# Four output projections as 64-row matmul pairs that change sides behind a wait on POOL

## Chip, core and metric

The kernel runs on one core of a Trainium2 chip. TensorE (PE) multiplies a stationary operand, loaded by a weight load (PEld), with a moving operand, and writes into one of eight PSUM banks; VectorE (DVE) and ScalarE (ACT) read PSUM; GpSimd (POOL) works beside them; SyncE (SP) issues most transfers. The metric is device microseconds (us) of one execution; lower is better.

## What is computed

Decayed linear attention over blocks of 64 positions (batch 2, 8 heads, 768 positions, head size 64), and then two feed-forward layers over its output x of 1536 tokens by 512. All are float32.

```python
h = x @ w_in                                   # 512 -> 2048
g = where(h >= 1, h, where(h <= -1, 0, (h + 1)**2 / 4))
x = g @ w_out                                  # 2048 -> 512
gate = 1 / (1 + exp(-(x @ w_gate)))            # 512 -> 1536
out = (gate * (x @ w_val)) @ w_out2            # 1536 -> 512
```

## The kernel before

Every float32 operand of a feed-forward matmul is split into a high and a low part (fp32r), and a product is three matmuls: high by high, high by low, low by high. The hidden width is cut into slices of 128: n = 0 to 15 of the first layer, n = 16 to 27 of the second (NF1 = 16, NF2 = 12). The 1536 tokens are three tiles t of 512 (NTT = 3). For each slice and tile the kernel makes the hidden values (gate and value products, tiles named h, p or t in the profile), their activation (gh, the high part, and gl, the low one), and then the output projection, `project`, which multiplies that slice's 512 tokens by its 128x512 piece w of the output weight.

A projection has four PSUM banks, accs[0] to accs[3] (a in the profile), one for each 128 tokens of the tile. For each bank it issues three matmuls of 128 rows, 128 columns of stationary operand and 512 moving columns: gh by w high, gh by w low, gl by w high. Two slices (GF = 2) accumulate into the same four banks; after the second one `flush` adds each bank to the tile `part[t]` in SBUF, one DVE addition of 128x512 per bank in the order j = 0 to 3 (L336), and for the last two slices SP sends each 128x512 piece to the output as soon as its addition is done (L339).

The banks of these accumulations come from a PSUM pool of four buffers, so that a projection of the next tile that starts anew (first) writes the same four banks, and each of its first matmuls waits for the DVE addition that reads that bank. The order on every engine is written out by hand. At the end of the program it is, on TensorE: the projections of slices 26 and 27 for tile 0, mixed with products; then, with nothing between them, (26, t=1), (27, t=1), (26, t=2), (27, t=2). Here (27, t=1) ends an accumulation and (26, t=2) begins the next one in the same four banks. After (27, t=2) come only four additions and four output transfers.

Two other parts of the program matter to the prediction. In the attention, `scores` (L980) multiplies operands of 64 rows for two heads, one in rows 0 to 63 and one in rows 64 to 127, in turn, each into a bank of its own; `values` (L1041) and `queries` (L1061) use the array in halves in other ways. And POOL makes sums of weights (L163) for the second layer, in a stretch that ends long before the last projections.

Of the kernel before, what the change touches and what calls it, by code (L numbers as in the profile page):

```python
# [15 lines left out]
B, H, S, D = 2, 8, 768, 64  # L16
# [9 lines left out]
NF1, NF2 = FF1 // P, FF2 // P  # L26
G0 = 4
GF = 2
# [17 lines left out]
def fused_kernel(ctx: ExitStack, tc: tile.TileContext, qkv, qd, cst, w1, w2, out):  # L46
    nc = tc.nc
    pe, act, dve, pool, sp = nc.tensor, nc.scalar, nc.vector, nc.gpsimd, nc.sync
# [10 lines left out]
    def bank(name, use="h"):  # L59
        pool_ = banks.get(use) or banks[None]  # L60
        return pool_.tile([P, 512], F32, tag="b", name=name)
# [178 lines left out]
    def w_need(n, o):  # L240
        while index[n, o] not in ws:
            k = prog["round"]
            w_round()
            assert prog["round"] > k
# [49 lines left out]
        dve.scalar_tensor_tensor(out=r, in0=r, scalar=1.0, in1=h, op0=ALU.min, op1=ALU.max)  # L294

    accs = {}

    def project(n, t, gs, first, last, now=True):
        gh, gl = gs
        two = n >= NF1  # L300
        o = 1024 if two else 512
        w_need(n, o)
        w = ws[index[n, o]]
        if first:
            accs.update({j: bank(f"a{n}_{t}_{j}", "a") for j in range(4)})
        for j in range(4):
            js = slice(j * P, (j + 1) * P)
            if two:
                ah, al = (g[j] if isinstance(g, list) else g[:, js] for g in (gh, gl))
                ops = [(ah, w[:, 0]), (ah, w[:, 1]), (al, w[:, 0])]  # L310
            else:
                ops = [(w[:, 0, js], gh), (w[:, 1, js], gh), (w[:, 0, js], gl)]
            for m, (a, b_) in enumerate(ops):
                pe.matmul(accs[j], lhsT=a, rhs=b_, start=(first and m == 0),  # L314
                          stop=(last and m == 2))
        if t == NTT - 1:
            used.update([index[n, o]] if two else [index[n, 0], index[n, o]])
        if last and now:
            flush(n, t)
# [4 lines left out]
    def flush(n, t, js=range(4)):  # L324
        two = n >= NF1
        begin = n == (NF1 + GF if two else G0) - 1
        end = n == (NF1 + NF2 if two else NF1) - 1
        for j in js:
            o = part[t][:, j]
            if begin:  # L330
                if j < 2 or (n, t) == (G0 - 1, 0):
                    act.activation(o, accs[j], AF.Copy)  # L332
                else:
                    dve.tensor_copy(out=o, in_=accs[j])
            else:
                dve.tensor_tensor(out=o, in0=o, in1=accs[j], op=ALU.add)  # L336
            if end and two:
                r0 = t * TT + j * P
                sp.dma_start(out=out[r0:r0 + P, :], in_=o)  # L339
# [24 lines left out]
    def feed_forward():  # L364
        def finish():
            project(*behind.pop(0))
            if u is not seq[-1]:
                w_round()
            if u in seq[4:6]:
                w_round()  # L370

        for u in seq:
            n, t, first, last = u
            h = hidden(n, t, 0)
            if u not in seq[1:G0]:
                split()
            yield
            r = act1(h, n, t)
            act1_end(r, h)
            fresh.append((u, r))  # L380
            yield
            j = seq.index(u)
            while attention_over and len(behind) >= (4 if j < NEARLY else 3 if j < 8 else 2):
                finish()
        split()
# [226 lines left out]
    def first_layer(waiting, made):  # L612

        square = lambda s: act.activation(s, s, AF.Square)
        for n0 in range(G0, NF1, GF):
# [18 lines left out]
            act1_end(s11, r[0])  # L634
            s22 = act1_begin(r[2], f"s{n1}_1")
            project(*waiting[0], now=False)
            square(s22)
            g11 = parts(s11, n0, 0)
            act1_end(s22, r[2])
            w_round()  # L640
            project(*waiting[1], now=False)
            g22 = parts(s22, n1, 1)
            t_ = waiting[1][:2]
# [185 lines left out]
    with ExitStack() as actx:  # L829
# [250 lines left out]
        with tc.manual_schedule():  # L1080
# [8 lines left out]
            for k in range(nu // 2):  # L1089
                a, b = 2 * k, 2 * k + 1  # L1090
# [79 lines left out]
    last = ctx.enter_context(ExitStack())  # L1170
# [80 lines left out]
```

## Time and profile before

| | |
|---|---|
| median of 3 runs | 583.23 us (583.21 to 583.51) |
| the profiled execution | 583.22 us |
| its span, first to last instruction | 581.4 us |
| TensorE busy in the span | 576.5 us, 99% |
| DVE, ACT, POOL busy | 78%, 66%, 9% |
| mean granted TensorE clock | 0.999 |

The span is what the trace shows; the profiled execution's own time is 1.8 us more. Busy time of PE is the union of its matmuls, which overlap: a matmul of 512 columns is listed with about 390 ns, but the next one starts sooner.

### The profile page before, as it was taken

What the parts mean: (1) busy time and instruction counts of PE and PEld (TensorE: products, weight loads), DVE (VectorE), ACT (ScalarE), POOL (GpSimd) and SP (SyncE); (2) the same over time, 40 slices, a digit from 0 to 9 for tenths busy, and PEclk for the clock granted to TensorE, in tenths of its full rate; (3) what the DMA queues carried; (4) which work ended last, traced back from release to release, by engine and by line L of the source; (5) the groups of instructions that cost most, each with busy time, mean ns of one, the idle gap of its engine ahead of it and who ended that gap; (6) DMA issues with size and microseconds to landing.
All of it is one profiled execution on the core that took longest, in us unless ns stands there. A gap on an engine that the chain in (4) does not pass through costs nothing.

```text
span 581.4 us, 8399 instructions
## 1 busy us (share of the span) xinstructions
PE 576.5 (99%) x3218; PEld 486.1 (84%) x3218; DVE 454.7 (78%) x772; ACT 383.4 (66%) x675; POOL 52.4 (9%) x60
## 2 busy tenths in 40 slices
PE   9999999999999999999999999999999999999997
PEld 8987888888888888888888888888888898898895
DVE  5988798788897978796898996688876676767555
ACT  4678785996777677777874977756655656655330
POOL 3440000000000000000000002422001112022000
PEclk9999999999999999999999999999999999999999
DMA  8983240022112222221312232222102221220014
GB/s 336 400 324 116 103 144 2 37 104 73 42 72 73 73 73 72 66 79 37 99 48 72 73 108 73 72 74 70 35 5 68 78 73 37 76 70 1 0 61 157
DMA packets 15880, 52.02 MB, mean 89 GB/s; under 512 B 1760, under 2 KB 1888, under 8 KB 15840
## 3 DMA queue, kind: packets, MB, share of 16 engines
q1 hardware_dynamic: 15696, 51.39, 25.1%
q8 instruction: 25, 0.41, 0.3%
q10 hardware_dynamic: 144, 0.10, 0.1%
q14 instruction: 15, 0.12, 0.1%
HBM read 48.33 MB, written 3.15 MB: 89 GB/s over the span
## 4 chain that ended last, share of the span: by engine, by line
PE 99%; DVE 0%; issue 0%
PE a L314 39%; PE p L502 26%; PE t L502 7%; PE h L258 6%; PE h L260 6%; PE h L259 6%; PE s L980 2%; PE x L1041 2%; PE x L1061 2%; PE uu L998 1%; PE z L889 1%; DVE part L336 0%; PE lam L897 0%; DVE zero L928 0%
## 5 line engine op out<-in xcount | busy, mean ns | idle before, releaser
L314 PE MATMUL a<-gh,w 128*128 128x512 f32 x384 | 118.4, 390 | 0.0
L314 PE MATMUL a<-w,gh 128*128 128x512 f32 x288 | 88.8, 390 | 0.0
L314 PEld LDWEIGHTS a<-gh,w 128*128 128x128 f32 x384 | 71.9, 188 | 15.3 <-ACT part L332 0.3
L336 DVE TENSOR_TENSOR part<-part,a 128x512 f32<-128x512 f32 x132 | 82.5, 681 | 2.7 <-PE a L314 2.7
L314 PE MATMUL a<-gl,w 128*128 128x512 f32 x192 | 74.7, 389 | 0.0
L258 PE MATMUL h<-xh,w 128*128 128x512 f32 x160 | 62.7, 392 | 0.0
L314 PEld LDWEIGHTS a<-w,gh 128*128 128x128 f32 x288 | 53.5, 188 | 10.7
L259 PE MATMUL h<-xh,w 128*128 128x512 f32 x160 | 62.3, 389 | 0.0
L260 PE MATMUL h<-xl,w 128*128 128x512 f32 x160 | 62.2, 389 | 0.0
L314 PE MATMUL a<-w,gl 128*128 128x512 f32 x144 | 56.0, 389 | 0.0
L124 ACT ACTIVATE wc<-raw 128x512 uint16<-128x512 uint32 x61 | 47.9, 785 | 10.5 <-DVE wr L135 10.5
L141 ACT ACTIVATE w<-wr 128x512 fp32r<-128x512 f32 x68 | 42.2, 621 | 16.8 <-DVE wr L135 16.6
L163 POOL TENSOR_TENSOR wr<-wr 128x256 f32<-128x256 f32 x16 | 13.3, 833 | 434.7 <-DVE w L145 434.1
L135 DVE CUSTOM_DVE_ANT_0 wr<-wr,wc 128x1024 uint16<-128x1024 uint16 x68 | 47.1, 692 | 5.8 <-ACT wc L125 3.2
L125 ACT ACTIVATE wc<-raw 128x512 f16<-128x512 f32 x61 | 46.9, 769 | 0.0
L145 DVE TENSOR_TENSOR w<-wr,w 128x512 fp32r<-128x512 f32 x65 | 45.2, 696 | 2.0 <-ACT w L141 1.7
L117 ACT ACTIVATE wr<-raw 128x512 f32<-128x512 f32 x68 | 45.0, 662 | 1.5 <-POOL s L172 0.9
L314 PEld LDWEIGHTS a<-gl,w 128*128 128x128 f32 x192 | 36.0, 188 | 7.5
L502 PE MATMUL p<-xh,s 128*128 128x512 f32 x128 | 39.5, 390 | 0.0
L502 PE MATMUL p<-xh,w 128*128 128x512 f32 x128 | 39.4, 389 | 0.0
L502 PE MATMUL p<-xth,s 128*128 128x512 f32 x128 | 39.4, 389 | 0.0
L258 PEld LDWEIGHTS h<-xh,w 128*128 128x128 f32 x160 | 30.0, 188 | 6.6 <-issue 0.2
(157 smaller groups left out, 1140.0 us busy)
## 6 DMA issues: line engine op xcount, KB each, us to landing
raw<-in_w SPq DMA_DIRECT2D x68, 512.0 KB, 3.4
u<-in_qkv SPq DMA_DIRECT2D x24, 384.0 KB, 8.2
out<-part SPq DMA_DIRECT2D x12, 256.0 KB, 2.1
u<-in_qkv SPq DMA_DIRECT2D x3, 768.0 KB, 8.6
part<-in_qkv SPq DMA_DIRECT2D x2, 384.0 KB, 8.4
cs<-in_cst ACTq DMA_DIRECT2D x1, 98.0 KB, 3.7
```

The costliest lines, as they stand in the source:

```text
L117: act.activation(r, hi.bitcast(F32), AF.Copy, scale=2.0 ** -112)
L124: act.activation(limb(U16)[:, :, 0], lo, AF.Copy, scale=2.0 ** -29)
L125: act.activation(limb(F16)[:, :, 1], hi.bitcast(F32), AF.Copy, scale=2.0 ** -60)
L135: eng.tensor_tensor(out=ri, in0=ri, in1=c, op=ALU.add)
L141: act.activation(ws[i][:, 0], tmps[i][0], AF.Copy)
L145: eng.tensor_tensor(out=ws[i][:, 1], in0=r, in1=ws[i][:, 0].bitcast(F32), op=ALU.subtract)
L258: pe.matmul(h, lhsT=wh, rhs=xh[:, k, tt], start=(k == 0), stop=False)
L259: pe.matmul(h, lhsT=wl, rhs=xh[:, k, tt], start=False, stop=False)
L260: pe.matmul(h, lhsT=wh, rhs=xl[:, k, tt], start=False, stop=(k == NP - 1))
L314: pe.matmul(accs[j], lhsT=a, rhs=b_, start=(first and m == 0), stop=(last and m == 2))
L336: dve.tensor_tensor(out=o, in0=o, in1=accs[j], op=ALU.add)
L502: pe.matmul(o, lhsT=a, rhs=b_, start=(start and k == 0 and m == 0), stop=(k == HK - 1 and m == 2), skip_group_check=True)
```

## The change

The condition `n >= NF1 + NF2 - GF and t` holds for the four projections (26, 1), (27, 1), (26, 2) and (27, 2). In them each matmul of 128 rows becomes two of 64 rows: rows 0 to 63 of both operands, and rows 64 to 127. The two halves of the array work for two different banks: in the first turn rows of one half go to bank 0 (then 2) and rows of the other to bank 1 (then 3), and in the second turn the halves are exchanged. A bank thus gets its sum from both halves of the array, one after the other. Slice 27 starts with the side on which slice 26 ended. Between the turns `relay` puts a wait: a POOL instruction without work waits for the last matmul of the bank pair's first turn, and the first matmul of its second turn waits for that POOL instruction. All other projections are as before.

```diff
+    def relay(first_, then=None):
+
+        sync = mybir.DependencyInfo(mybir.DependencyClass.Sync, mybir.DependencyReason.DATA)
+        if then is None:
+            step = pool.nop()
+            tc.add_manual_dep(step.ins, first_.ins.name, sync, reason="row tile done")
+            return step
+        tc.add_manual_dep(then.ins, first_.ins.name, sync, reason="bank changes its row tile")
...
+        if n >= NF1 + NF2 - GF and t:
+            done = []
+            for turn in range(2):
+                for js in ((0, 1), (2, 3)):
+                    for m in range(3):
+                        for e, j in enumerate(js):
+                            half_ = turn ^ e ^ (n & 1)
+                            r = slice(half_ * D, (half_ + 1) * D)
+                            a, b_ = ops[j][m]
+                            ins = pe.matmul(accs[j], lhsT=a[r], rhs=b_[r],
+                                            start=(first and turn == 0 and m == 0),
+                                            stop=(last and turn == 1 and m == 2))
+                            if turn and m == 0 and e == 0:
+                                relay(done[j // 2], ins)
+                            if not turn and m == 2 and e == 1:
+                                done.append(relay(ins))
+        else:
+            for j in range(4):
+                for m, (a, b_) in enumerate(ops[j]):
+                    pe.matmul(accs[j], lhsT=a, rhs=b_, start=(first and m == 0),
+                              stop=(last and m == 2))
```

The first place is on TensorE, where projection (27, t=1) ends and (26, t=2) begins. In the names a26_1_3 is bank 3 of tile 1 and a26_2_0 bank 0 of tile 2; the bracket tells which engine's semaphore the matmul waits for, and x2 that two equal ones follow each other. Before:

```order
L314 MATMUL a26_1_2_5504<-w67_5251,gh27_1_5386 128x512 x2
L314 MATMUL a26_1_2_5504<-w67_5251,gl27_1_5388 128x512
L314 MATMUL a26_1_3_5505<-w67_5251,gh27_1_5386 128x512 x2
L314 MATMUL a26_1_3_5505<-w67_5251,gl27_1_5388 128x512
L314 MATMUL a26_2_0_5540<-w66_5232,gh26_0_5494 128x512 [waits DVE_49,Activation_49]
L314 MATMUL a26_2_0_5540<-w66_5232,gh26_0_5494 128x512
L314 MATMUL a26_2_0_5540<-w66_5232,gl26_0_5496 128x512
L314 MATMUL a26_2_1_5541<-w66_5232,gh26_0_5494 128x512 [waits DVE_49]
```

With the change, the same place on TensorE, from the last two pairs of (27, t=1) on:

```order
L331 MATMUL a26_1_2_5504<-w67_5251,gh27_1_5386 128x512
L331 MATMUL a26_1_3_5505<-w67_5251,gh27_1_5386 128x512
L331 MATMUL a26_1_2_5504<-w67_5251,gl27_1_5388 128x512
L331 MATMUL a26_1_3_5505<-w67_5251,gl27_1_5388 128x512
L331 MATMUL a26_2_0_5568<-w66_5232,gh26_0_5494 128x512 [waits DVE_49,Activation_49]
L331 MATMUL a26_2_1_5569<-w66_5232,gh26_0_5494 128x512 [waits DVE_49]
L331 MATMUL a26_2_0_5568<-w66_5232,gh26_0_5494 128x512
L331 MATMUL a26_2_1_5569<-w66_5232,gh26_0_5494 128x512
L331 MATMUL a26_2_0_5568<-w66_5232,gl26_0_5496 128x512
L331 MATMUL a26_2_1_5569<-w66_5232,gl26_0_5496 128x512
L331 MATMUL a26_2_2_5570<-w66_5232,gh26_1_5495 128x512 [waits DVE_49,Activation_49]
L331 MATMUL a26_2_3_5571<-w66_5232,gh26_1_5495 128x512 [waits DVE_49]
```

Banks 2 and 3 of tile 1 now end together, and the first two matmuls of tile 2 wait for the additions of two banks, where before there were three matmuls of one bank between two such waits. The order on DVE is unchanged.

The second place is the middle of the last projection, (27, t=2), on TensorE with the change, where the banks change sides:

```order
L331 MATMUL a26_2_2_5570<-w67_5251,gl26_1_5497 128x512
L331 MATMUL a26_2_3_5571<-w67_5251,gl26_1_5497 128x512
L331 MATMUL a26_2_0_5568<-w67_5251,gh26_0_5494 128x512 [waits Pool_sequencer_49]
L331 MATMUL a26_2_1_5569<-w67_5251,gh26_0_5494 128x512
L331 MATMUL a26_2_0_5568<-w67_5251,gh26_0_5494 128x512
L331 MATMUL a26_2_1_5569<-w67_5251,gh26_0_5494 128x512
L331 MATMUL a26_2_0_5568<-w67_5251,gl26_0_5496 128x512
L331 MATMUL a26_2_1_5569<-w67_5251,gl26_0_5496 128x512
L331 MATMUL a26_2_2_5570<-w67_5251,gh26_1_5495 128x512 [waits Pool_sequencer_49]
```

Before, a bank was finished by three matmuls in a row and no matmul here waited for POOL; now banks 0 and 1 are finished six matmuls before the end, and banks 2 and 3 with the last two.

## Rows read from the trace of the kernel before

**Rows 1.** The page's parts 1 and 2: busy us, share, instructions; granted clock.

```profile
PE 576.5 (99%) x3218; PEld 486.1 (84%) x3218; DVE 454.7 (78%) x772; ACT 383.4 (66%) x675; POOL 52.4 (9%) x60
...
PEclk9999999999999999999999999999999999999999
```

**Rows 2.** The page's part 4, the chain that ended last, by engine.

```profile
PE 99%; DVE 0%; issue 0%
```

**Rows 3.** Busy time by window: us, then each engine's busy us, clock, DMA.

```profile
566.50:572.00 5.50, 5.50 (x27) 4.54 (x26) 4.42 (x7) 1.51 (x3) 0.00 (x0) 1.00 0.20 76
572.00:577.60 5.60, 5.59 (x25) 4.32 (x23) 2.89 (x5) 0.00 (x0) 0.00 (x0) 1.00 0.53 199
```

**Rows 4.** Timeline of PE: last 256-column products, first matmuls of (26, t=1).

```profile
566.29 0.28 PE L502 MATMUL t<-xh,s 128*128 128x256 f32 x1
566.41 0.28 PE L502 MATMUL t<-xl,s 128*128 128x256 f32 x1
566.53 0.63 PE L314 MATMUL a<-w,gh 128*128 128x512 f32 x2
567.00 0.39 PE L314 MATMUL a<-w,gl 128*128 128x512 f32 x1
567.22 0.63 PE L314 MATMUL a<-w,gh 128*128 128x512 f32 x2
```

**Rows 5.** Timeline of PE, projection (27, t=1) from its first matmul.

```profile
569.27 0.62 PE L314 MATMUL a<-w,gh 128*128 128x512 f32 x2
569.73 0.39 PE L314 MATMUL a<-w,gl 128*128 128x512 f32 x1
569.95 0.62 PE L314 MATMUL a<-w,gh 128*128 128x512 f32 x2
```

**Rows 6.** Timeline of DVE behind it: the four additions of tile 1.

```profile
569.56 0.69 DVE L686 TENSOR_TENSOR gl<-v,gh 128x512 fp32r<-128x512 f32 x1 [0.76 <-ACT gh L695]
570.17 2.71 DVE L336 TENSOR_TENSOR part<-part,a 128x512 f32<-128x512 f32 x4
```

**Rows 7.** Timeline from 572: start of (26, t=2), third and last matmul of (27, t=2).

```profile
571.99 0.62 PE L314 MATMUL a<-w,gh 128*128 128x512 f32 x2
...
575.17 0.39 PE L314 MATMUL a<-w,gl 128*128 128x512 f32 x1
...
577.21 0.39 PE L314 MATMUL a<-w,gl 128*128 128x512 f32 x1
```

**Rows 8.** Timeline of DVE: the last four additions.

```profile
575.59 2.73 DVE L336 TENSOR_TENSOR part<-part,a 128x512 f32<-128x512 f32 x4 [2.71 <-PE a L314]
```

**Rows 9.** The tile out, from 570 us on: the last eight output transfers.

```profile
L339 SPq DMA_DIRECT2D out<-part x8: 332/332/333, 570.9 to 578.3; - x8
...
DMA to landing us min/median/max: 2.0/2.1/2.1
```

**Rows 10.** Line L980, scores: ns min/median/max, first and last start, rows*columns.

```profile
L980 PEld LDWEIGHTS s<-u x180: 182/188/334, 4.8 to 42.9; 64*128 64x128 f32 x180
L980 PE MATMUL s<-u x180: 271/272/580, 4.8 to 43.0; 64*128 64x128 f32 x180
```

**Rows 11.** Timeline of PE in scores, from four windows: whole run, pieces of another.

```profile
28.83 1.61 PE L980 MATMUL s<-u 64*128 64x128 f32 x24
...
33.75 0.38 PE L980 MATMUL s<-u 64*128 64x128 f32 x2
...
34.30 0.61 PE L980 MATMUL s<-u 64*128 64x128 f32 x8
...
35.08 0.28 PE L980 MATMUL s<-u 64*128 64x128 f32 x2
```

**Rows 12.** Timeline of PE at a change from whole array to halves.

```profile
39.07 0.39 PE L259 MATMUL h<-xh,w 128*128 128x512 f32 x1
39.30 0.39 PE L260 MATMUL h<-xl,w 128*128 128x512 f32 x1
39.62 0.33 PE L1041 MATMUL x<-pT,u 128*64 128x128 f32 x2
```

**Rows 13.** Timeline, two hand-overs: ACT to a weight load, ACT to POOL.

```profile
78.84 0.57 ACT L332 ACTIVATE part<-a 128x512 f32<-128x512 f32 x1
79.46 0.30 PEld L314 LDWEIGHTS a<-gh,w 128*128 128x128 f32 x2 [0.28 <-ACT part L332]
...
34.10 0.63 ACT L141 ACTIVATE w<-wr 128x512 fp32r<-128x512 f32 x1 [0.98 <-DVE wr L135]
34.81 1.29 POOL L145 TENSOR_TENSOR w<-wr,w 128x512 fp32r<-128x512 f32 x1 [5.12 <-ACT w L141]
```

**Rows 14.** POOL: its semaphore instructions at the program's end; its sums, mean ns.

```profile
L1247 POOLq EVENT_SEMAPHORE  x4: 17/17/17, 580.7 to 581.3; - x4
...
L163 POOL TENSOR_TENSOR wr<-wr 128x256 f32<-128x256 f32 x16 | 13.3, 833 | 434.7 <-DVE w L145 434.1
```

**Rows 15.** Windows behind the last matmul: columns as in rows 3.

```profile
578.60:579.60 1.00, 0.00 (x0) 0.00 (x0) 0.00 (x0) 0.00 (x0) 0.00 (x0) 1.00 1.03 387
579.60:580.60 1.00, 0.00 (x0) 0.00 (x0) 0.00 (x0) 0.00 (x0) 0.00 (x0) 1.00 0.32 119
580.60:581.40 0.80, 0.00 (x0) 0.00 (x0) 0.00 (x0) 0.00 (x0) 0.00 (x0) 0.52 0.00 0
```

More of the change, by code (lines that the diff above doesn't have):

```diff
@@ L305, in project @@
             accs.update({j: bank(f"a{n}_{t}_{j}", "a") for j in range(4)})
+        ops = {}
         for j in range(4):
@@ L309, in project @@
                 ah, al = (g[j] if isinstance(g, list) else g[:, js] for g in (gh, gl))
-                ops = [(ah, w[:, 0]), (ah, w[:, 1]), (al, w[:, 0])]
+                ops[j] = [(ah, w[:, 0]), (ah, w[:, 1]), (al, w[:, 0])]
             else:
[L312 to L315, printed above, removed]
+                ops[j] = [(w[:, 0, js], gh), (w[:, 1, js], gh), (w[:, 0, js], gl)]
+        if n >= NF1 + NF2 - GF and t:
[19 more added lines that the diff above has]
+                              stop=(last and m == 2))
         if t == NTT - 1:
```

## The prediction, made before the change was run

> **What bounds the kernel now.** The page's busy times come first: TensorE is busy in 576.5 of 581.4 us, at the full clock in every slice [rows 1], and the chain that ended last lies on TensorE for 99% [rows 2]. So the windows of the last stretch, where the change lies: TensorE is busy in 5.50 of 5.50 us and then 5.59 of 5.60, POOL has nothing, and the clock is 1.00 [rows 3]. Nothing waits ahead of TensorE there; whatever it gains or loses is time. The timeline gives the step of a matmul, from start to start, which counts and not its 0.39 us: (27, t=1) has three matmuls of 512 columns in 569.95 - 569.27 = 0.68 us [rows 5], 0.227 each. With 256 columns the step is 0.12 us [rows 4]. So 256 columns more cost 0.107, a 512-column stream takes 0.213, and 0.013 is fixed. The four projections are 48 steps, 10.9 us.
>
> Behind TensorE comes DVE. An addition takes 0.68 us when four follow each other (2.71 us and 2.73 us for four [rows 6, 8]), just what three matmuls take. Today banks finish one by one, 0.68 us apart, and the additions keep pace: those of (27, t=1) begin at 570.17, behind its third matmul (569.73 + 0.39 = 570.12), and the first bank is free long before (26, t=2) begins at 571.99 [rows 5 to 7]. At the end the last matmul ends at 577.21 + 0.39 = 577.60 and the last addition at 575.59 + 2.73 = 578.32, 0.72 us later [rows 7, 8]; the output transfers behind it take the same with the change [rows 9].
>
> **Part 1, the matmuls themselves: 0.** 48 matmuls become 96, as 48 pairs. Do the two of a pair run side by side? The nearest rows are those of `scores`, which uses the same two halves in turn, into two banks. There 24 matmuls of 0.272 us take 1.61 us; the last pair, two matmuls of 0.272, together takes 0.28, so its starts are 0.01 apart; and eight take 0.61, so that the step of a pair is (0.61 - 0.27) / 3 = 0.113 [rows 10, 11]. The two run side by side, and so do the two 128-column weight loads of 0.188 us that each 0.113 us step contains [rows 10, 11]. I carry that over: a pair of 512 columns has the step of one matmul of 512, 0.227. Below, the fixed part could shrink to the 0.006 that scores has over 0.107, a saving of 48 x 0.007 = 0.3 us (0.4 if the rounding is against me); above, the 0.01 between two starts could add to every step, up to 0.4 us.
>
> Here a rule can be held against the row. The Trainium skill (TensorE: Matmul & The Clock Gate, LDWEIGHTS) says that a load's time goes by its columns, about columns / 1.2 ns, and not by its rows: half-row loads save nothing (the trace agrees that rows don't help: 0.188 us with 64 rows), and two in turn would be 0.213 us by an estimate from that page, still hidden behind a step. By the 0.188 us of a row, two in turn would be 0.376, and 48 steps 7.2 us longer. The scores rows, with two loads per 0.113 us, exclude the second here.
>
> **Part 2, the array changes from whole to halves, once: 0.19 us.** At such a change the step to the next matmul was 39.62 - 39.30 = 0.32 in place of 0.227 [rows 12], 0.09 more; and the first pair of scores behind a change lasts 0.38 in place of 0.28, its first load having been hidden by nothing [rows 11], 0.10 more. It happens where (26, t=1) begins. The program ends in halves, so there is no way back.
>
> **Part 3, eight waits through POOL: 0.** Number the pairs of a projection 0 to 11. Pair 6 waits for the end of pair 2. That end is 0.39 us behind its start, and the load of pair 6 would start with pair 5, three steps = 0.68 us behind it: 0.29 us are free. The relay is three hops. TensorE to a waiting engine takes 0.03 (575.17 + 0.39 = 575.56, the addition starts at 575.59 [rows 7, 8]); ACT to POOL 0.08 (34.73 to 34.81) and ACT to a weight load 0.05 (79.41 to 79.46) [rows 13]; POOL's semaphore instructions take 0.017 [rows 14]. Together 0.13 to 0.16: hidden behind pairs 3 to 5. An instruction without work is nearest to those 0.017; were it as slow as a POOL sum, 0.83 [rows 14], the relay would take about 0.96 and each projection would lose 0.67 at its pair 6 (pair 9 is then late by as much, and its wait hidden): 2.7 us in all. POOL has nothing else queued then [rows 3].
>
> **Part 4, the banks come free later: 1.73 us.** This is what the new order costs. In (27, t=1) banks 0 and 1 now finish together with pair 8, banks 2 and 3 with pair 11. Move the projection's start to 569.27 + 0.19 = 569.46. Pair 8 starts at 571.27, ends at 571.66, and the four additions begin at 571.70 (before: 570.17) and end at 572.39, 573.07, 573.75 and 574.43. (26, t=2) would begin at 571.99 + 0.19 = 572.18. Its first matmul needs bank 0, its second bank 1, and a load that waited starts 0.05 us behind its releaser; its matmul loses another 0.11 (load at 79.46, the next at 79.46 + 0.30 - 0.19 = 79.57 [rows 13]). So the second starts at 573.07 + 0.16 = 573.23, and everything queued behind it waits too. Pair 3 needs banks 2 and 3: the second of it starts at 574.43 + 0.16 = 574.59, where without waits pair 3 would start at 572.18 + 0.68 = 572.86. TensorE is late by 1.73 us, and nothing covers it: behind it stand only the rest of (26, t=2) and (27, t=2).
>
> **Part 5, the tail: 1.25 us.** In (27, t=2) the same happens behind the last matmul. Banks 0 and 1 are ready 0.68 us ahead of the end, and four additions take 2.73: the last ends 0.03 + 2.73 - 0.68 = 2.08 us behind the last matmul, against 0.72, so 1.36 more. The stall of part 4 may let the first matmul of each pair run a step ahead of its partner, since it waits for the earlier bank; then bank 0 is ready 0.23 earlier, and the tail costs 1.13. Whether the relays keep that lead is close (it takes 0.23 of their 0.29 us), so I take the middle.
>
> Sum: 0 + 0.19 + 0 + 1.73 + 1.25 = 3.17 us on the profiled execution's 583.22 (span 581.4 and 1.8 around it), which is the median but for 0.01: **586.4 us**, 0.5% slower. A measurement of this kernel can tell about 0.2%, 1.2 us, from no change. With the bounds of parts 1 and 5 this case reaches from 585.8 to 587.0.
>
> **The rivals.**
> - *The relay shows.* POOL's step is slow and pair 6 waits in each projection. For it: the trace has no hand-over through POOL back to TensorE. Against it: the 0.017 us rows. At the bound, 586.4 + 2.7 = 589.1.
> - *Pairs share, but not fully.* Each pair takes more than a whole matmul, since two moving streams and two banks are served. For it: scores' 0.113 was with 128 columns of plain float32, not 512 of fp32r. Against it: its two starts within 0.01. With a step 30% longer, 0.295, the pairs cost 48 x 0.068 = 3.3 us; by the arithmetic of parts 4 and 5 the longer steps give DVE more time, and the waits fall to 1.25 and the tail to about 1.0: 583.22 + 3.3 + 0.19 + 1.25 + 1.0 = 589.0. The Trainium skill (TensorE: Matmul & The Clock Gate, Part 3) measured 3.07 and not 4 times the speed for four row tiles, which by an estimate from that page would be a step of this size; no row of this trace has four.
> - *The change doesn't do what it says:* halves run one after the other. 48 x 0.227 = 10.9 us more; additions then keep pace in the middle, and the tail costs 0.44: 10.9 + 0.19 + 0.44 gives 594.7. Scores speaks against it.
> - *The clock falls* in the stalls of part 4, from 573 on. The remaining 23 steps at half the clock cost 23 x 0.213 = 4.9 us, of which about 1 hides the waits: about 590. Against it: behind the last matmul TensorE is idle from 577.60, and the windows up to 580.60 still show 1.00, only the one behind it 0.52 [rows 15]; the longest pause here is about 0.5 us.
> - *Not slower:* a pair streams faster than a whole matmul, because a half has half the rows to pass. The place is all 48 steps. It decides where a step falls below 0.227 - 3.17 / 48 = 0.161 us. For it: scores' 0.113. Against it: that is for 128 columns, and 512 columns stream in 0.213 here. At 0.12, 48 x 0.107 = 5.1 us are saved: 581.3.
>
> **Chances.** The forecast 0.73, relay 0.08, partial sharing 0.08, one after the other 0.05, clock 0.03, not slower 0.03. The range reaches from below the forecast's own lower bound (585.6) to the two rivals at 589.1: 0.73 + 0.16 = 0.89 less the edges of each. Slower by over 0.2% is all but the last case and what little of the forecast could shrink below 584.4: 0.95; within 0.2%: 0.02; faster: 0.03.
>
> **What will show it.** The profile after should list pairs in the last projections with starts 0.01 apart and a step of 0.22 to 0.23 us; one PE step of about 0.42 at (26, t=1); no idle time ahead of the pairs that wait for POOL; weight loads of (26, t=2) that wait for DVE's L363 additions, about 1 us at its start and 0.7 at its fourth pair; the four last additions back to back, ending about 2 us behind the last matmul; and a clock of 1.00. The prediction is wrong where the step of a pair is another, above all, since it is multiplied by 48, or where the first matmuls of (26, t=2) don't wait.

## The result, and the profile after

The changed kernel takes 586.75 us (median of 4 runs, 586.00 to 588.07); the kernel before takes 583.37 (4 runs, 583.21 to 583.51). The ratio is 1.006, with an interval of 1.004 to 1.0081. The same kernel run again beside the experiments gave 586.30 us (5 runs, 585.86 to 586.48), a ratio of 1.0051 (1.0039 to 1.0064). The second set ran because the first four times spread over 2 us; if that spread was not the kernel's own, 586.2 us with a spread of 0.5 was expected, and the spread is 0.6. The change makes the kernel slower by about 3 us, with 586.4 predicted. The profiled execution has a span of 584.4 us against 581.4. Its own time of 588.07 is the longest of the four: it has 3.67 us outside the span where the kernel before had 1.82. So what follows is an account of the 3.0 us of the span, landmark by landmark.

The page of the changed kernel first: busy time by engine and the granted clock in 40 slices.

```profile
PE 578.0 (99%) x3266; PEld 486.4 (83%) x3266; DVE 454.3 (78%) x772; ACT 383.6 (66%) x675; POOL 52.4 (9%) x60
...
PEclk9999999999999999999999999999999999999999
```

Against [rows 1], TensorE has 48 matmuls more and is busy 1.5 us longer, and the clock is full in every slice. The other 1.5 us of the 3.0 are time in which TensorE is not busy. Next comes the timeline of TensorE where the halves begin.

```profile
566.31 0.40 PE L529 MATMUL t<-xh,s 128*128 128x256 f32 x2
566.55 0.28 PE L529 MATMUL t<-xl,s 128*128 128x256 f32 x1
566.76 0.73 PE L331 MATMUL a<-w,gh 64*128 64x512 f32 x4
567.33 0.39 PE L331 MATMUL a<-w,gl 64*128 64x512 f32 x2
567.56 0.63 PE L331 MATMUL a<-w,gh 64*128 64x512 f32 x4
568.02 0.39 PE L331 MATMUL a<-w,gl 64*128 64x512 f32 x2
568.25 0.62 PE L331 MATMUL a<-w,gh 64*128 64x512 f32 x4
568.70 0.39 PE L331 MATMUL a<-w,gl 64*128 64x512 f32 x2
```

A group "x2" is one pair, and it lasts 0.39 us, as long as one of its matmuls alone (next fence): the two run side by side. From 568.02 to 568.70 lie three pairs, so the step of a pair is 0.68 / 3 = 0.227 us, that of a whole matmul in [rows 5]. The change of the array shows twice: 566.76 - 566.55 = 0.21 in place of 0.12, and the first two pairs last 0.73 where later ones last 0.62 and 0.63. Together that is 0.19 to 0.20. The last 256-column matmul itself starts 0.14 later than in [rows 4]; that lies ahead of the change, and the same landmark lies between 566.30 and 566.83 in the kernels below.

Now the line of the half matmuls (ns min/median/max, first and last start), what its loads waited for (us, times), and POOL's instruction for the wait.

```profile
L331 PEld LDWEIGHTS a<-w,gh x64: 182/184/187, 566.8 to 578.6; 64*128 64x128 f32 x64
L331 PE MATMUL a<-w,gh x64: 383/386/501, 566.8 to 578.8; 64*128 64x512 f32 x64
...
  DVE part L363: 0.9, 3
  issue: 0.6, 1
```
```profile
L301 POOLq EVENT_SEMAPHORE  x8: 17/17/17, 567.8 to 578.1; - x8
```

POOL takes 17 ns for each of the eight waits, and none of them is among what the loads waited for. In the first projection pair 2 ends at 567.72 and POOL acts at 567.76; the load that needs it comes at 568.03, just with the pair ahead of it, so 0.26 us were to spare. What the loads do wait for is DVE. The next two fences show the four additions of tile 1 and the weight loads of (26, t=2).

```profile
571.85 2.48 DVE L363 TENSOR_TENSOR part<-part,a 128x512 f32<-128x512 f32 x4 [1.45 <-PE a L331]
```
```profile
572.65 0.18 PEld L331 LDWEIGHTS a<-w,gh 64*128 64x128 f32 x1 [0.58 <-issue]
573.18 0.29 PEld L331 LDWEIGHTS a<-w,gh 64*128 64x128 f32 x3 [0.35 <-DVE part L363]
573.30 0.42 PEld L331 LDWEIGHTS a<-w,gl 64*128 64x128 f32 x2
573.85 0.18 PEld L331 LDWEIGHTS a<-w,gh 64*128 64x128 f32 x1
574.38 0.29 PEld L331 LDWEIGHTS a<-w,gh 64*128 64x128 f32 x3 [0.35 <-DVE part L363]
```

The additions begin at 571.85, where [rows 6] had 570.17, and start 0.60 us apart: (2.48 - 0.68) / 3. Each pair of banks holds TensorE up: the load at 572.65 follows the first addition, those at 573.18, 573.85 and 574.38 the next three. The profile puts the first wait down to "issue" and has no bracket at 573.85, but each of the four follows the end of its addition (572.53, 573.13, 573.73 and 574.33) by 0.05 to 0.12 us. The load of the second matmul of the fourth pair (pair 3) starts at 574.38, and its matmul gets under way 0.11 us later, at 574.49 (it is listed from 574.38 on, with 0.50 us in place of 0.39). The last pair of tile 1 starts at 572.10, so that without waits pair 3 would have started four steps later, at 573.01: TensorE is 1.48 us late. The windows show the same, with the clock at 1.00 (columns as in [rows 3]).

```profile
566.50:572.10 5.60, 5.60 (x49) 4.54 (x50) 2.92 (x5) 1.65 (x3) 0.00 (x0) 1.00 0.18 66
572.10:574.60 2.50, 2.24 (x13) 1.07 (x11) 2.23 (x4) 0.00 (x0) 0.00 (x0) 1.00 0.49 184
574.60:579.40 4.80, 4.80 (x41) 4.06 (x39) 0.79 (x2) 0.00 (x0) 0.00 (x0) 1.00 0.33 123
```

In the 2.50 us of the middle row 13 matmuls run, two of them begun before it; at a pair every 0.227 us 22 would start. TensorE is still called busy for 2.24 of the 2.50 us, since a matmul's 0.39 us covers much of a pause behind it. That is why the engine's share of busy time hides this stall, and only starts tell it. Last, the end: the timeline, and the tile `out`.

```profile
578.61 2.48 DVE L363 TENSOR_TENSOR part<-part,a 128x512 f32<-128x512 f32 x4 [4.29 <-PE a L331]
...
578.87 0.56 PE L331 MATMUL a<-w,gl 64*128 64x512 f32 x2
579.33 2.12 SPq L366 DMA_DIRECT2D out<-part  x4
```
```profile
L366 SPq DMA_DIRECT2D out<-part x4: 332/333/333, 579.3 to 581.1; - x4
...
DMA to landing us min/median/max: 2.0/2.2/2.3
```

The last matmul ends at 578.87 + 0.56 = 579.43 and the last addition at 578.61 + 2.48 = 581.09, 1.66 us later, against 0.72 [rows 7, 8]: 0.94 more. The last pair's two matmuls start 0.18 apart (0.56 for two, 0.39 for one), so most of the lead that the stall gave to the first of each pair is kept to the end. The output transfers now leave 0.60 us apart instead of 0.68, and the last lands 2.28 us after its issue, against 2.04 (2.0 to 2.1 in [rows 9]): another 0.24. What holds it stands in the windows over these transfers.

```profile
580.40:581.40 1.00, 0.00 (x0) 0.00 (x0) 0.69 (x2) 0.00 (x0) 0.00 (x0) 1.00 1.04 385
581.40:582.40 1.00, 0.00 (x0) 0.00 (x0) 0.00 (x0) 0.00 (x0) 0.00 (x0) 1.00 1.03 385
```

In both windows the 16 DMA engines are busy all the time (share 1.03 to 1.04) and move 385 GB/s (387 in [rows 15]). At that rate a transfer of 256 KB (262,144 bytes) takes 0.68 us. The transfers are issued every 0.60 us, so the fourth has fallen 3 x 0.08 = 0.24 us behind. The sum is 0.14 + 0.19 + 1.48 + 0.94 + 0.24 = 2.99 us of the span's 3.0.

### The profile page after: what moved, and what is told of

It reads as the page before. It is cut to its first block, busy times and chain, and to the rows that moved or that the text cites. A ratio compares the mean times of both kernels' runs of the same rounds, so it can differ in the third digit from the quotient of the medians.

```text
span 584.4 us, 8504 instructions
## 1 busy us (share of the span) xinstructions
PE 578.0 (99%) x3266; PEld 486.4 (83%) x3266; DVE 454.3 (78%) x772; ACT 383.6 (66%) x675; POOL 52.4 (9%) x60
## 4 chain that ended last, share of the span: by engine, by line
PE 98%; DMA 1%; DVE 0%; SPq 0%; DVEq 0%; issue 0%; POOL 0%; POOLq 0%
PE a L341 37%; PE p L529 26%; PE t L529 7%; PE h L258 6%; PE h L260 6%; PE h L259 6%; PE x L1068 2%; PE s L1007 2%; PE a L331 2%; PE x L1088 2%; PE uu L1025 1%; DMA u<-in_qkv 1%; DVE part L363 0%; SPq L887 0%; DVEq L1274 0%
## 5 line engine op out<-in xcount | busy, mean ns | idle before, releaser
L341 PE MATMUL a<-w,gh 128*128 128x512 f32 x256 | 78.9, 390 | 0.0
L341 PEld LDWEIGHTS a<-w,gh 128*128 128x128 f32 x256 | 47.6, 188 | 9.5
L341 PE MATMUL a<-w,gl 128*128 128x512 f32 x128 | 49.8, 389 | 0.0
```

## The experiments

The kernels before beside which they ran took 583.35 us (runs 1 to 4) and 583.29 (the others).

**1. The order alone.** Whole rows, each bank's matmuls in an order that finishes banks about when the pairs do; no halves, no waits through POOL.

```diff
-            done = []
-            for turn in range(2):
...
+            turns = {j: 0 for j in range(4)}
+            for j in (0, 1, 0, 2, 3, 2, 1, 0, 1, 3, 2, 3):
+                m = turns[j]
+                turns[j] += 1
+                a, b_ = ops[j][m]
+                pe.matmul(accs[j], lhsT=a, rhs=b_, start=(first and m == 0),
+                          stop=(last and m == 2))
```

> Whole-row matmuls, no halves and no waits through POOL, but the four banks are taken in an order in which banks 0 and 1 end eight and nine matmuls into a projection, banks 2 and 3 with the last two. Theory A (the loss is the late release of banks and the late start of the additions and outputs): a stall of about 1.0 us where tile 2 begins and 1.1 to 1.2 us at the end, so span 583.6, time about 585.4. Theory B (the halves, their mode change or the waits through POOL cost the time): as before the change, span 581.4, time 583.3.

Measured: 585.45 us (585.32 to 585.48), ratio 1.0037 (1.0024 to 1.0049), span 583.6. Its weight loads wait, over the last 17 us (us in all, times, longest):

```profile
PEld a L328 <- issue: 0.7, 2, 0.4
PEld a L328 <- DVE part L355: 0.7, 2, 0.3
```

About two thirds of the loss (2.1 of about 3 us) are there without a single half row. The order in which banks finish and are wanted is enough; how the array is split is not needed for it.

**2 and 3. One tile each.** Halves in tile 2 alone, then in tile 1 alone.

```diff
-        if n >= NF1 + NF2 - GF and t:
+        if n >= NF1 + NF2 - GF and t == 2:
```

> Halves and waits through POOL in the two projections of tile 2 alone; those of tile 1 as before. Theory A: no stall where tile 2 begins, since tile 1's banks end one by one; 0.2 us for the change to halves and 1.2 us at the end stay: span 582.8, time about 584.6. Theory B (a cost per pair or per wait): half of the whole change's 3.0 us, span 582.9 as well, but spread over the 24 pairs, whose step would then have to be 0.06 us above 0.227.

> Halves and waits in the two projections of tile 1 alone; tile 2 as before, bank by bank. Theory A: the end is as before, the change to halves and back costs 0.2 us each way, and the first bank of tile 2 is waited for by 0.1 to 0.3 us, the later ones not: span 581.9 to 582.1, time about 583.8. Theory B: half of 3.0 us, span 582.9, time about 584.8.

Measured: tile 2 alone 584.82 us (584.61 to 584.95), ratio 1.0026 (1.0015 to 1.0036), span 583.2; tile 1 alone 583.78 (583.62 to 584.08), ratio 1.0008 (0.9999 to 1.0017), span 582.1. In the spans that is 1.8 + 0.7 = 2.5 us, short of the 3.0 of both together, and in the medians 1.47 + 0.43 = 1.90, against 3.01 in the second set of the changed kernel, though the array changes three times in the two and once in the whole. One weight load waits in each over the last 17 us; tile 2 alone, then tile 1 alone:

```profile
PEld a L331 <- issue: 0.4, 1, 0.4
```
```profile
PEld a L341 <- issue: 0.6, 1, 0.6
```

The first wait is at the change of the array. The second is for the addition of bank 0, the first of the four waits of the changed kernel; the other three are gone. So most of the stall belongs to neither tile alone: (26, t=2) must want two banks at once, and (27, t=1) must free them late. Tile 2 alone pays the tail, tile 1 alone little. The span of tile 2 alone, 583.2, is 0.4 above what I expected; about 0.2 of it is the later landing of the last output, which I had left out.

**4. Other banks.** The whole change, but (26, t=2) takes its four banks from the pool that `h` used, so that it needs not wait for tile 1's additions.

```diff
+            use = "h" if n == NF1 + NF2 - GF and t == 2 else "a"
-            accs.update({j: bank(f"a{n}_{t}_{j}", "a") for j in range(4)})
+            accs.update({j: bank(f"a{n}_{t}_{j}", use) for j in range(4)})
```

> The whole change, but tile 2's sums go to the four banks of the other PSUM pool, which nobody reads any more, in place of those that the additions of tile 1 are still reading. Theory A: the stall of 1.5 us where tile 2 begins is gone and nothing else moves: span 582.9, time about 584.7, and in the trace no weight load of slice 26, tile 2 waits for an addition. Theory B: the span stays at 584.4.

Measured: 584.80 us (584.45 to 585.58), ratio 1.0029 (1.0019 to 1.0039), span 583.0. Its windows over both tiles, and its last additions:

```profile
566.70:572.20 5.50, 5.50 (x49) 4.57 (x50) 3.11 (x5) 1.37 (x3) 0.00 (x0) 1.00 0.12 46
572.20:577.80 5.60, 5.60 (x50) 4.33 (x48) 2.64 (x5) 0.00 (x0) 0.00 (x0) 1.00 0.50 187
```
```profile
577.21 2.48 DVE L364 TENSOR_TENSOR part<-part,a 128x512 f32<-128x512 f32 x4 [2.96 <-PE a L332]
...
577.47 0.39 PE L332 MATMUL a<-w,gl 64*128 64x512 f32 x2
```

The additions of tile 1 take just as long and begin as late, but now nobody waits for them: 50 matmuls run in the second window's 5.60 us, and TensorE is busy in all of it. The stall is gone, and 1.4 us of the span with it. Without a stall there is no lead either (the last pair lasts 0.39 us), and so the tail is longer: 577.21 + 2.48 - (577.47 + 0.39) = 1.83 us.

**5. Other banks, and the last projection in whole rows.** As 4, and (27, t=2) runs as before.

```diff
-        if n >= NF1 + NF2 - GF and t:
+        if n >= NF1 + NF2 - GF and t and (n, t) != (NF1 + NF2 - 1, 2):
```

> Tile 2's sums in the other pool's banks, and the very last projection in whole rows, bank by bank, as before; halves and waits in the three projections ahead of it. Theory A: no stall where tile 2 begins, the additions and outputs at the end as before, only the change to halves and back is left, 0.2 us each: span 581.8, time about 583.7. Theory B (a cost per pair or wait): three quarters of 3.0 us: span 583.6, time about 585.5.

Measured: 583.66 us (583.45 to 583.83), ratio 1.0007 (0.9998 to 1.0016), span 581.7. Its last additions:

```profile
575.90 2.76 DVE L364 TENSOR_TENSOR part<-part,a 128x512 f32<-128x512 f32 x4 [1.82 <-PE a L342]
```

They end at 578.66, 0.73 us behind the last matmul (577.54 + 0.39 = 577.93), as before the change. Three projections still run as 36 pairs with their waits, and cost nothing that the measurement tells from no change. What is left, 0.3 us of the span, is not more than the two changes of the array were expected to cost (0.4). So the stall and the tail, with the outputs behind it, are the loss.

**6 and 8. A slower step in the relay.** POOL sets a small tile and adds it to itself, twice (6) or once (8), where it had an instruction without work.

```diff
-            step = pool.nop()
+            step = pool.memset(idle, 0.0)
...
+            for _ in range(2):
+                step = pool.tensor_tensor(out=idle, in0=idle, in1=idle, op=ALU.add)
```

> The whole change, but POOL's step between the two turns is work: a memset and two additions of 128x127 in place of an instruction without work, by the page's POOL rows about 1.0 us in place of 0.02. If the waits through POOL are hidden by about 0.3 us of slack in the changed kernel, each of the four projections now loses what exceeds it, 0.7 to 0.9 us: 2.8 to 3.6 us more than the changed kernel, span 587.2 to 588.0. If the relay had much more cover, little is added, span 584.4 to 585.

> As the slow relay, with a memset and one addition of 128x127 on POOL, by the slow relay's trace 0.7 us from the first one's start to the second one's end. In the changed kernel POOL's empty instruction starts 0.26 us ahead of the load that waits for it, so 0.7 us of work should make the load 0.5 us late, once in each of four projections (the second wait of a projection is then late by as much anyhow): 2.0 us more than the changed kernel, span 586.2 to 586.6, if the clock stays at its full level. If the second wait counts too, or the clock falls as in the slow relay, more: 588 and over.

Measured: with two additions 592.43 us (591.42 to 593.02), ratio 1.0155 (1.0141 to 1.0169), span 590.3, outside what was expected; with one 588.19 (588.10 to 588.23), ratio 1.0084 (1.0066 to 1.0102), span 586.4, inside it. The waits of the weight loads, of 6 and then of 8:

```profile
PEld a L334 <- POOL half L305: 6.8, 8, 1.3
PEld a L334 <- DVE part L366: 0.7, 2, 0.4
```
```profile
PEld a L334 <- POOL half L305: 3.0, 7, 0.6
```

My expectation for 6 had the second wait of each projection hidden behind the first. All eight show: POOL's steps take 1.2 us each (the first two 1.5) and follow one another, while the two matmuls they answer lie 0.68 us apart, so the second is later still. In run 8 seven waits show, but only four of them, of 0.55 to 0.61 us and one in each projection, hold TensorE up, as expected; behind the other three, of 0.21 to 0.27, its matmuls keep their step. In the profiled execution of run 6 the clock fell as well: its windows and timeline.

```profile
571.00:574.00 3.00, 3.00 (x16) 2.32 (x14) 0.00 (x0) 0.00 (x0) 0.40 (x2) 0.50 0.00 0
575.00:577.00 2.00, 1.76 (x13) 0.88 (x11) 1.27 (x3) 0.00 (x0) 0.79 (x2) 1.00 0.00 0
```
```profile
571.90 1.06 PE L334 MATMUL a<-w,gh 64*128 64x512 f32 x4
572.75 0.63 PE L334 MATMUL a<-w,gl 64*128 64x512 f32 x2
573.18 1.06 PE L334 MATMUL a<-w,gh 64*128 64x512 f32 x4
```

At a granted clock of 0.50 (1.2 of 2.4 GHz) three pairs take 573.18 - 571.90 = 1.28 us, 0.43 each. Another execution of run 6 has a mean clock of 1.000 and still a span of 589.5, 5.1 us above the changed kernel's, so the waits are most of the loss. So the relay's rival and the clock's are both real ways to lose time in this place, and the changed kernel stays clear of both: its waits through POOL don't show, and its clock is 1.00.

**7. The waits alone.** Whole rows in the order of before, with the eight waits through POOL put between the banks.

```diff
+                    if j > 1 and m == 0:
+                        relay(done[j - 2], ins)
+                    if j < 2 and m == 2:
+                        done.append(relay(ins))
```

> Whole rows in the order of before, and eight waits through POOL without work, each from the end of one bank's matmuls to the first matmul of the bank after next. Theory A: each wait has three steps of cover, nothing is lost: span 581.4, time 583.3. If a wait through POOL costs time of its own, even when it is over early, 8 of them show: 0.1 us each would be span 582.2.

Measured: 583.29 us (583.08 to 583.56), ratio 0.9999 (0.999 to 1.0008). A relay with three steps of cover costs nothing.

**9. Two output transfers less.** As 4, without the first two of tile 2's four output transfers.

```diff
-            if end and two:
+            if end and two and (t < NTT - 1 or j > 1):
```

> Tile 2's sums in the other banks, as in the earlier run, and the first two of tile 2's four output transfers left out, so that half of that tile's output is not written; the additions stay. If the end is set by the four transfers queueing on the way out (they follow each other in 0.60 us and the last lands 2.3 us behind its issue, before the change 2.06), the last one now lands in about 2.06 us, the span is 0.2 us less than with all four, 582.8. If it is the last addition and a fixed time behind it, the span stays at 583.0 and the landing at 2.3 us.

Measured: 585.11 us (584.74 to 585.85), ratio 1.0032 (1.0019 to 1.0045), span 582.9 against 583.0 in run 4. The landings of run 4, then of this one:

```profile
DMA to landing us min/median/max: 2.0/2.2/2.3
```
```profile
DMA to landing us min/median/max: 2.0/2.1/2.1
```

Without two transfers ahead of it the last one lands 0.16 us sooner (2.11 us after its issue in the trace, against 2.27 in run 4), which is two of the 0.08 us that each transfer falls behind. The 2.06 of the expectation belongs to an earlier transfer; the last one before the change has 2.04. The end of the span did not follow: it lies 3.23 us behind the last addition, against 3.26 in run 4 and 3.04 before the change. In every other trace the span ends 0.96 or 0.97 us behind the last landing, here 1.09, and why stays open. So neither expectation is met: the transfers do wait for one another, but this run doesn't show the program ending sooner when they wait less.

## Why the prediction was right, and where its terms were off

**Part 1 (0) holds.** The step of a pair is 0.227 us, and run 5 has 36 pairs at no cost. Neither bound showed: no smaller fixed part and no 0.01 more for each pair. Two half loads of 0.184 us each fit in a step of 0.227, so they overlap. The partial sharing that the prediction drew from the Trainium skill (TensorE: Matmul & The Clock Gate, Part 3), where four row tiles gave 3.07 times the speed, does not show with two; no run here has four.

**Part 2 (0.19) holds** at 0.19 to 0.20, in the two places that were named.

**Part 3 (0) holds,** by POOL's 17 ns, by 0.26 us to spare in the trace, and by run 7.

**Part 4 (1.73) had the right mechanism and a size too large: 1.48.** The mis-sized term is the addition. The prediction said that "an addition takes 0.68 us when four follow each other", from [rows 6] and [rows 8]. But there each addition waits for its bank's three matmuls, which take 0.68: the rows show TensorE's pace. With all banks ready, DVE starts an addition every 0.60 us: (2.48 - 0.68) / 3, in the changed kernel and in runs 1 to 4 where banks end in pairs. The fourth is then 3 x 0.08 = 0.24 us sooner, and 1.73 - 0.24 = 1.49. A hint stood beside the rows: 2.73 us for four is four times 0.68, and a chain that leaves no gap at all and keeps exactly another engine's pace may be bound by that engine. More than a hint stood in the same trace, in tile 0, whose additions begin late behind other work of DVE, so that each finds its bank ready. Its four additions, and the landings of its four outputs, before the change:

```profile
563.00 2.48 DVE L336 TENSOR_TENSOR part<-part,a 128x512 f32<-128x512 f32 x4
```
```profile
DMA to landing us min/median/max: 2.0/2.2/2.3
```

Both the 0.60 us and the later landings could have been read there. Runs 1, 2, 3 and 4 show that the full stall needs both tiles in the new order and the same banks.

**Part 5 (1.25) was off for the same reason: 0.94.** Its bounds, 1.13 with the lead and 1.36 without, become 0.89 and 1.12 with 0.60 us for an addition. The changed kernel, which keeps the lead, measured 0.94; run 4, which has none, 1.83 - 0.72 = 1.11. The middle was the wrong choice: the relays keep most of the lead, 0.18 of 0.23 us.

**"The output transfers behind it take the same with the change" was wrong by 0.24 us.** They leave closer together and the last lands later. This error and that of part 5 cancel for a reason: behind the last matmul the faster additions gain 0.24 us, and the transfers, which need 0.68 us each at 385 GB/s, give it back. From the last matmul to the end the changed kernel takes 0.94 + 0.24 = 1.18 us longer, which is part 5's own arithmetic with the 0.18 of lead that was kept: 1.36 - 0.18. So the prediction's 1.25 was nearly right for the end of the program, but by luck: its 0.68 us is the pace of the transfers, and it had put it down to the additions. In sum, part 4 was 0.25 too much, the end 0.07 too much, and the 0.14 ahead of the change, which is no part of it, was missing: 3.17 against 2.99.

Of the rivals, one after the other, partial sharing and a gain from faster pairs are excluded by the step of 0.227 us. The relay and the clock were shown to be possible, by run 6, and absent from the changed kernel. What the prediction held against the clock's fall, that 3 us of rest at the end of the program left it at 1.00, is weaker than it looked: in run 6 the clock fell behind waits of 1.34 and 1.01 us.

What stays open: the time outside the span. In the nine executions of the changed kernel it is 1.74 to 3.67 us, in the 49 of the kernel before that ran beside the experiments 1.77 to 2.02. Runs 4, 6 and 9, which also end in halves, reach 2.3 to 3.3, but runs 2 and 8, which end in halves too, stay at 1.75 to 2.02. Nothing in the traces shows why, and the two medians of the changed kernel, 586.75 and 586.30, differ by more than their spans do.

## What to carry to other kernels

When a split lets two banks be summed side by side, ask when each bank is finished and when the next work wants it: work that finishes in pairs hands its banks over late and wants them early, and both costs (a stall in the middle, a tail at the end) are paid even where the split itself is free. Other banks remove the stall, and the old order for the last group removes the tail. The time that a chain of instructions takes is its own only where its inputs were all ready; if its spacing equals that of the engine that feeds it, look for another place in the trace, where the inputs wait for it (here tile 0). And when a chain gets faster, ask what takes over the pace behind it: here the output transfers took back at the end what the additions had gained.

## What the runs showed of the hardware

- Two matmuls of 64 rows and 512 columns run fully side by side, loads included: 0.227 us for a pair, as for one matmul of 128 rows (forecast in part 1).
- Additions of 128x512 from PSUM start 0.60 us apart with their inputs ready, though each is listed at 0.68 (2.48 us for four).
- In run 6 the granted clock stood at 0.50 from 570.96 to 574.37, behind two waits of weight loads of 1.34 and 1.01 us; later waits of 1.08 and 0.68 us in the same run, and waits of 0.58 and 0.35 us in the changed kernel, left it at 1.00.
- Output transfers of 256 KB take 0.68 us each at the 385 GB/s that the 16 engines moved when busy all the time; issued 0.60 us apart, the fourth lands 2.28 us after its issue, where it was 2.04 at 0.68 apart.
